# Wider records for the routing lists: rows of 64 bytes in DRAM in place of rows of 16

## The chip, the cores and the metric

The kernel runs on one core of one Trainium2 chip. The metric is the time of one execution on the device in microseconds (us). Before the change three runs took 736.26, 739.16 and 739.34 us; their median, 739.16 us, is the time before. The engines are named as in the profile: PE is TensorE, DVE is VectorE, ACT is ScalarE, POOL is GpSimd, SP is SyncE, which here only issues transfers. SPq, ACTq and POOLq are the instruction queues of those engines where they issue transfers.

## The reference

The inputs are q, k, v (4 batches, 8 heads, 576 positions, 64 wide) and the weights of two feed-forward layers. Three stages follow one another, all in float32:

```python
# 1 attention: heads 0-3 see the last 32 positions, heads 4-7 every fourth of the last 128
scores = np.where(mask, q @ k.T / 8, -1e9);  attn = softmax(scores);  x = attn @ v      # x: 2304 tokens x 512
# 2 experts: each token goes to the one expert of 8 with the largest logit
e_idx = argmax(x @ w_gate);  gate = softmax(x @ w_gate)[e_idx];  eom = sigmoid(x @ w_output_gate)
out[mask_e] = gate * eom[:, e] * (relu(x[mask_e] @ w1[e]) @ w2[e])                       # 512 -> 1024 -> 512
# 3 dense layer
h = relu(out @ w_in);  result = (h * h) @ w_out                                          # 512 -> 2048 -> 512
```

The experts run on gathered tokens: the kernel must know for every expert which tokens are its own, and with what factor.

## The kernel before, in words

**The attention stage** (function `attention`) walks over 18 tiles of 128 tokens. A loop runs over the first 15 tiles (L649), the last three are written out by hand behind it (L699 to L764). Each step of the loop loads later tiles of q, k and v on SP's queue (`load_q`, `load_k`, `load_v`), multiplies q with k (`qk`, L433), subtracts the row maximum on POOL (L454), takes the exponential on ACT (`ex`, L459), transposes (`tr`, L466), multiplies with v (`pv`, L482), normalizes on DVE (L492 to L498) and transposes the result for the gate (`xt`, L520). From step 9 on finished rows of x are stored to DRAM (`store`, L512 and L514, tensor `x_d`).

**Routing.** The tiles are taken in six groups (`GROUPS`). At the end of a group `lg` and `route1` to `route6` find each token's expert, its rank within that expert's list and its factor. `scatter` (L624) then writes one record per token into the DRAM tensor `meta_d`, which holds eight lists of MS = 2560 rows, one list per expert. A record is four 32-bit words: the token's number, the factor's bits, the token's number again, and a word not used. It is written by an indirect store on POOL's queue: a column of up to 128 tokens (one per partition) is one instruction, and the vector `di` holds for each the row of `meta_d` that it goes to. There are 20 such stores, spread over the attention stage. Their source is `idsb`, a part of the constants' tile `late_sb`, in which the token numbers lie ready and into which `route5` writes the factors (L611).

Before the first record is written, `clear` (L409) fills all of `meta_d` with zeros and, in the third word, the number OOB, so that rows that no token takes lead nowhere. It is one transfer of 320 KB on SP's queue, from a tile that POOL has filled (L642, L643), issued in the loop's step 3. The first `scatter` waits until it has landed.

**The experts stage** (function `experts`) works through nine windows, one or two per expert, in an order that is found at run time. Records are read in three places:

- `meta_load` (L153) reads a window's records into SBUF, one record per partition, and `gather` (L158) fetches the tokens' rows of x by them, with an indirect load on POOL's queue.
- `ids_out` (L855) copies a window's records from `meta_d` to the DRAM tensor `idc_d`, in the order of the experts' outputs. It is issued on ACT's queue, after the fourth of the eight `up` steps of a window (after the whole window for the first two).
- `spilled` (L1454) would read them for tokens that found no place in a window. Here it has nothing to do.

After the last window one transfer on SP's queue (L1086) reads `idc_d` into SBUF, and the 18 indirect stores of the final result (L1431) take their rows from it.

In each window `up` multiplies with w1 (12 matmuls into one of three PSUM banks `hp`, L829, then ACT and DVE take the bank out, L834 and L835) and `down` with w2 (L844, five banks `yp`). The weights come in pieces of 512 KB (`load_w`, at most three on the way, in the three `raw` buffers) and are split by ACT and DVE (`conv_w`, L143 and L144) one window ahead of their use.

**The order of the work** is written out by hand. All transfers of one issuing engine are issued in program order, and an instruction that waits holds up those behind it on its engine.

Of the kernel before, what the change touches and what calls it, by code (L numbers as in the profile page):

```python
# [13 lines left out]
I32 = mybir.dt.int32  # L14
# [9 lines left out]
P = 128  # L24
# [7 lines left out]
NG = len(GROUPS)  # L32
# [3 lines left out]
E = 8  # L36
# [5 lines left out]

HALF = EARLY * P // E
MS = NT + 256
YC = sum(WIN) + 192
NEG = -8.0e9
OOB = 65535
# [21 lines left out]
def attention_experts_kernel(ctx: ExitStack, tc: tile.TileContext, qB, kB, vB, wE, wF, consts, late, rows, out):  # L69
    nc = tc.nc  # L70
    cpool = ctx.enter_context(tc.tile_pool(name="cpool", bufs=1))
    dpool = ctx.enter_context(tc.tile_pool(name="dpool", bufs=1, space=DRAM))
# [2 lines left out]
    stg = stg_st.enter_context(tc.tile_pool(name="stg", bufs=1, side="right"))  # L75

    x_d = dpool.tile([NT, DM], F32, name="x_d")
    meta_d = dpool.tile([E * MS, 4], I32, name="meta_d")
    yT_d = dpool.tile([DM, YC], F32, name="yT_d")
    idc_d = dpool.tile([YC, 4], I32, name="idc_d")  # L80
    g_d = [dpool.tile([FF2, TP], F32, name=f"g_d{i}") for i in range(NTP)]
# [7 lines left out]
    w8 = late_sb[:, 2 * P:2 * P + 4 * E].rearrange("p (a e) -> p a e", e=E)  # L89
    eoff = late_sb[:, 2 * P + 4 * E:2 * P + 8 * E].rearrange("p (a e) -> p a e", e=E)  # L90
    idsb = late_sb[:, 2 * P + 8 * E:].bitcast(I32).rearrange("p (g b c) -> p g b c", b=4, c=4)
    cum = cpool.tile([P, NG + 1, E], BF16, name="cum")
    idc = cpool.tile([P, NT // P, 4], I32, name="idc")
    rowc = cpool.tile([1, 4 * E + E * E + NSPILL], F32, name="rowc")
# [8 lines left out]
    mt = cpool.tile([P, E + 1, 3, 4], I32, name="mt")  # L103
# [5 lines left out]
    def raw_tile():  # L109
        return stg.tile([P, 1024], F32, tag="raw", name="raw", bufs=3)  # L110
# [16 lines left out]
    reg = {}  # L127
# [25 lines left out]
    def meta_load(w, engine=None, n="p"):  # L153
        r, s0, _ = WD[w]
        k = len(tiles(w))
        (engine or nc.gpsimd).dma_start(out=mt[:, w, 0:k], in_=meta_d[ds(reg[n, r] * MS + s0, P * k), :].rearrange("(i p) c -> p i c", p=P))

    def gather(w):  # L158
        known = (NB if w else EARLY) * P
# [166 lines left out]
    def attention():  # L326
# [77 lines left out]
            nc.sync.dma_start(out=late_sb, in_=late)  # L404
            nc.sync.dma_start(out=rowc, in_=rows)

        z = raw_tile().bitcast(I32)[:, 0:MS * E * 4 // P].rearrange("p (n c) -> p n c", c=4)

        def clear():  # L409
            nc.sync.dma_start(out=meta_d.rearrange("(p n) c -> p n c", p=P), in_=z)  # L410

        sm_t, p_t, pt_t, o_t, x_t, xT_t, lg_t = {}, {}, {}, {}, {}, {}, {}

# [179 lines left out]
        def route5(g):  # L593

            ls, e, oh = rt[g]
            rk = rk_t.pop(g)
            n, c = rows_of(g), COLS[g]
            m = idsb[:, g, 0:c]
            v = nc.vector
            zp, z, ez, se, dn = t3(g, "zp"), t2(g, "z"), t2(g, "ez"), t2(g, "se"), t2(g, "dn")  # L600
            r1, s2, di = t3(g, "r1"), t2(g, "s2"), wk.tile([P, 4], I32, tag="di", name="di", bufs=4)[:, 0:c]
            v.tensor_tensor(out=zp[n], in0=oh[n], in1=ls[n, :, E:2 * E], op=ALU.mult)
            v.reduce_sum(out=se[n], in_=e[n], axis=AX.X)
            v.reduce_sum(out=z[n], in_=zp[n], axis=AX.X)
            nc.scalar.activation(out=ez[n], in_=z[n], func=ACTF.Exp, scale=-1.0)
            v.tensor_tensor(out=r1[n], in0=rk[n, 0:c], in1=eoff[n, 0:c], op=ALU.add)
            v.tensor_scalar(out=se[n], in0=se[n], scalar1=1e-9, scalar2=None, op0=ALU.add)
            v.tensor_tensor(out=r1[n], in0=r1[n], in1=oh[n], op=ALU.mult)
            v.scalar_tensor_tensor(out=dn[n], in0=ez[n], scalar=1.0, in1=se[n], op0=ALU.add, op1=ALU.mult)
            v.reduce_sum(out=s2[n], in_=r1[n], axis=AX.X)  # L610
            v.reciprocal(out=m[n, :, 1:2].bitcast(F32), in_=dn[n].unsqueeze(2))  # L611
            v.tensor_copy(di[n], s2[n])
            rt[g] = di, m, oh
# [26 lines left out]
            clear_v(j, 1, nc.gpsimd)  # L640
        nc.gpsimd.memset(cum, 0.0)
        nc.gpsimd.memset(z, 0)  # L642
        nc.gpsimd.memset(z[:, :, 2:3], OOB)  # L643
        ex(0)
        load_q(4, 2)
        load_v(2, 2)
# [2 lines left out]
        for i in range(EARLY):  # L649
            tr(i)  # L650
            ex(i + 1)
            qk(i + 2)
            t = (i + 2) % LAP
            n = i + 2 - t + LAP
            if t == 2 and n < NB:
                load_k(n, 2)
            if t == 4 and n + 2 < NB:
                wrap()
                load_k(n + 2, min(3, NB - n - 2))

            if i % 2 == 0 and i + 6 < NB:
                load_q(i + 6, 2)
            if i == 0:
                load_consts()
            if i == 3:
                clear()
            if i == 3:
                nc.vector.tensor_copy(tri, tri32)
                nc.vector.tensor_copy(cs[:, 0, :], io8)
            for a, g in ((2, ends.get(i - 2)), (4, ends.get(i - 3))):  # L670
                if g is not None and g < NG - 3:
                    scatter(g, range(a - 2, min(a, COLS[g])))
            if i > 0:
                xt(i - 1)
            g = ends.get(i - 1)
            if g is not None:
                route4(g)
            pv(i)
            if i == 0:
                for j in range(4, VR):  # L680
                    clear_v(j, 0, nc.vector)
                    clear_v(j, 1, nc.gpsimd)
                load_v(4, 2)
            if i % 2 == 1 and i + VR - 1 < NB:
                load_v(i + VR - 1, 2)
            for a in STORES.get(i, ()):
                store(a, 2)
            if i in ends:
                lg(ends[i])
                route1(ends[i])  # L690
                route2(ends[i])
                route3(ends[i])
            if g is not None:
                route5(g)
                route6(g)
                if g == NG - 3:
                    scatter(g)

        i, g = EARLY, NG - 2  # L699
# [54 lines left out]
        for t in tiles(0):  # L754
            scale(0, t)
            j, n = t
# [4 lines left out]
        n = WD[0][2]  # L761
# [4 lines left out]
    def experts():  # L766
# [88 lines left out]
        def ids_out(w):  # L855
            r, s0, n = WD[w]
            at = slice(HALF * w, HALF * w + n) if w < 2 else ds(oa[r], n)
            nc.scalar.dma_start(out=idc_d[at, :], in_=meta_d[ds(reg["a", r] * MS + s0, n), :])

# [112 lines left out]
        for w in range(NW):  # L974
            at = {i: [] for i in range(12)}
# [478 lines left out]
    def spilled():  # L1454
# [5 lines left out]
        with ExitStack() as st:  # L1460
            sp = st.enter_context(tc.tile_pool(name="sp", bufs=1))
            ps = st.enter_context(tc.tile_pool(name="sps", bufs=2, space=PSUM))
            with tc.For_i(0, total) as i:
                ev = loaded(spill[:, 0, ds(i, 1)], mybir.EngineType.SP, E - 1, "cut to the experts")[0]
                rv = loaded(spill[:, 1, ds(i, 1)], mybir.EngineType.SP, E * MS - P, "cut to the rows")[0]
                m = sp.tile([P, 4], I32, name="m")
                nc.sync.dma_start(out=m, in_=meta_d[ds(rv, P), :])
                x = sp.tile([P, DM], F32, name="sx")
                nc.gpsimd.indirect_dma_start(
                    out=x, out_offset=None, in_=x_d,  # L1470
# [5 lines left out]
                p = ps.tile([P, 4, P], F32, tag="a", name="sa")  # L1476
# [10 lines left out]
                for c in range(4):  # L1487
                    w = load_w(c).rearrange("p (k f) -> p k f", k=4)
                    for f in range(2):
                        p = ps.tile([P, P], F32, tag="a", name="sa")  # L1490
# [4 lines left out]
                for c in range(4):  # L1495
                    w = load_w(4 + c).rearrange("p (k d) -> p k d", k=8)
                    p = ps.tile([P, P], F32, tag="a", name="sa")
# [4 lines left out]
                for f in range(16):  # L1502
                    w = []
# [6 lines left out]
                    p = ps.tile([P, P], F32, tag="a", name="sa")  # L1510
                    for k in range(4):
                        nc.tensor.matmul(out=p, lhsT=wi[:, k, :], rhs=y[:, k, :], start=(k == 0), stop=(k == 3))
                    r = sp.tile([P, P], F32, tag="r", name="sr", bufs=2)
# [102 lines left out]
```

## Time and profile before

| | |
|---|---|
| median of 3 runs | 739.16 us |
| the profiled execution | 733.13 us, of which the span is 731.5 us |
| PE busy | 696.5 us (95%) |
| DVE, ACT, POOL busy | 488.0 (67%), 327.6 (45%), 116.5 us (16%) |
| transfers | 136.90 MB, 187 GB/s on average |

The profile is one execution, taken by the hardware profiler. The time outside the span is 1.6 us. The granted clock is that of TensorE, 1.00 being the upper of its two levels (2.4 GHz) and 0.50 the lower (1.2 GHz). The attention stage lasts to about 110 us of the span, the experts stage to about 350 us, the dense layer to the end. A row of the timeline view gives the start, the duration, the engine, the line, the operation, and in brackets for how long the engine had been idle before it and which work ended that wait; "issue" means that the engine waited for nothing that the profile shows.

### The profile page before, as it was taken

The page shows a single profiled execution, that of the slowest core. Times are in us where ns is not written, and L with a number is a line of the kernel's source. Part 1 is how long each engine was busy: PE and PEld are TensorE (multiplying, and loading weights), DVE is VectorE, ACT ScalarE, POOL GpSimd, SP SyncE. Part 2 cuts the span into 40 slices and gives each one's busy share as a digit, 9 for nine tenths or more (in the row PEclk, how much of TensorE's full clock was granted, in tenths as well). Part 3 has the DMA queues.
Part 4 walks back from the last instruction along what each step waited for, and adds up shares of the span by engine and source line. Part 5 has one row for each costly group of instructions (what it writes and reads, how often), then busy time and mean ns, then how long its engine had stood idle before and what let it go on. Part 6 is the DMA issues. An engine that isn't in the chain of part 4 may idle for free. (4 is left out here: it accounts for less than half of the span.)

```text
span 731.5 us, 13885 instructions
## 1 busy us (share of the span) xinstructions
PE 696.5 (95%) x5227; PEld 633.6 (87%) x5227; DVE 488.0 (67%) x898; ACT 327.6 (45%) x601; POOL 116.5 (16%) x122
## 2 busy tenths in 40 slices
PE   7978759999999999999999999999999999999995
PEld 4766529999999999999999999999988888888884
DVE  7867636677566476677986877777888854445441
ACT  2544415454455555666655555465444422222120
POOL 6354434320110101006200000000000030003003
PEclk9999869999999999999999999999999999999998
DMA  8988475673756668673537645557655443235302
GB/s 286 394 231 248 140 225 167 205 253 133 229 188 204 207 179 261 212 238 95 201 129 252 202 172 201 176 201 241 222 194 193 137 155 127 87 112 169 108 23 90
DMA packets 62307, 136.90 MB, mean 187 GB/s; under 512 B 10361, under 2 KB 37242, under 8 KB 61210
## 3 DMA queue, kind: packets, MB, share of 16 engines
q1 hardware_dynamic: 52586, 120.09, 51.1%
q0 software_dynamic: 4176, 10.57, 4.2%
q10 hardware_dynamic: 5472, 5.29, 2.1%
q8 instruction: 43, 0.70, 0.4%
q14 instruction: 30, 0.25, 0.1%
HBM read 102.00 MB, written 33.96 MB: 186 GB/s over the span
## 5 line engine op out<-in xcount | busy, mean ns | idle before, releaser
L1386 DVE TENSOR_TENSOR slot_d<-gq,slot_d 128x768 fp32r<-128x768 f32 x48 | 45.9, 957 | 63.4 <-ACT slot_d L1384 63.4
L1384 ACT CAST slot_d<-gq 128x768 fp32r<-128x768 f32 x48 | 40.0, 836 | 97.5 <-PE op L1422 90.0
L1431 POOL DMA_INDIRECT out<-os,idc x18 | 19.8, 1100 | 353.2 <-DVE os L1430 348.9
L162 POOL DMA_INDIRECT xg<-x_d,mt x23 | 25.6, 1115 | 140.6 <-PE xp L186 95.1
L834 ACT ACTIVATE hh<-hp 128x240 fp32r<-128x240 f32 (+6 forms) x72 | 29.2, 407 | 40.6 <-PE hp L822 40.0
L1377 DVE SCALAR_TENSOR_TENSOR gq<-gq 128x768 f32<-128x768 f32 x48 | 45.6, 951 | 1.0 <-DMA gq<-g_d 1.0
L144 DVE TENSOR_TENSOR slot_d<-raw,slot_d 128x1024 fp32r<-128x1024 f32 x24 | 29.3, 1226 | 19.6 <-ACT slot_d L143 19.6
L1423 PE MATMUL op<-slot_a,slot_d 128*128 128x512 f32 x108 | 42.0, 389 | 0.0
L1422 PE MATMUL op<-slot_b,slot_d 128*128 128x512 f32 x108 | 42.0, 389 | 0.0
L1423 PE MATMUL op<-slot_b,slot_d 128*128 128x512 f32 x108 | 42.0, 389 | 0.0
L1422 PE MATMUL op<-slot_a,slot_d 128*128 128x512 f32 x108 | 42.0, 389 | 0.0
L1421 PE MATMUL op<-slot_b,slot_d 128*128 128x512 f32 x108 | 42.0, 389 | 0.0
L1421 PE MATMUL op<-slot_a,slot_d 128*128 128x512 f32 x108 | 42.0, 389 | 0.0
L835 DVE SCALAR_TENSOR_TENSOR hl<-hp,hh 128x240 fp32r<-128x240 f32 (+6 forms) x72 | 31.3, 444 | 12.9 <-ACT hh L834 12.8
L849 ACT COPY ys<-yp 128x240 f32<-128x240 f32 (+6 forms) x36 | 14.2, 396 | 46.3 <-PE yp L822 43.3
L144 DVE TENSOR_TENSOR slot_b<-raw,slot_b 128x1024 fp32r<-128x1024 f32 x20 | 24.3, 1222 | 12.5 <-ACT slot_b L143 12.5
L820 PE MATMUL yp<-hh,slot_b 128*128 128x240 f32 (+3 forms) x112 | 31.9, 285 | 0.0
L821 PE MATMUL yp<-hl,slot_b 128*128 128x240 f32 (+3 forms) x112 | 31.7, 283 | 0.0
L822 PE MATMUL yp<-hh,slot_b 128*128 128x240 f32 (+3 forms) x112 | 31.6, 282 | 0.0
L144 DVE TENSOR_TENSOR slot_a<-raw,slot_a 128x1024 fp32r<-128x1024 f32 x15 | 18.3, 1223 | 18.8 <-ACT slot_a L143 18.8
L820 PE MATMUL hp<-xh,slot_d 128*128 128x384 f32 (+3 forms) x96 | 29.7, 310 | 0.0
L821 PE MATMUL hp<-xl,slot_d 128*128 128x384 f32 (+3 forms) x96 | 29.7, 309 | 0.0
(323 smaller groups left out, 2301.6 us busy)
## 6 DMA issues: line engine op xcount, KB each, us to landing
raw<-in_wE SPq DMA_DIRECT2D x63, 512.0 KB, 4.0
g_d<-cr SPq DMA_DIRECT2D x96, 192.0 KB, 2.3
gq<-g_d SPq DMA_DIRECT2D x48, 384.0 KB, 3.0
raw<-in_wF SPq DMA_DIRECT2D x32, 512.0 KB, 3.6
vb<-in_vB SPq DMA_DIRECT2D x16, 520.0 KB, 5.6
yr<-yT_d SPq DMA_DIRECT2D x16, 384.0 KB, 6.9
q<-in_qB SPq DMA_DIRECT2D x8, 512.0 KB, 7.2
x_d<-x SPq DMA_DIRECT2D x22, 128.0 KB, 6.7
```

The costliest lines, as they stand in the source:

```text
L144: nc.vector.tensor_tensor(out=lo, in0=raw, in1=hi.bitcast(F32), op=ALU.subtract)
L820: nc.tensor.matmul(out=out, lhsT=wh, rhs=mh, start=first, stop=False, skip_group_check=shared)
L821: nc.tensor.matmul(out=out, lhsT=wh, rhs=ml, start=False, stop=False, skip_group_check=shared)
L822: nc.tensor.matmul(out=out, lhsT=wl, rhs=mh, start=False, stop=last, skip_group_check=shared)
L834: nc.scalar.activation(out=h[:, :n], in_=p[:, :n], func=ACTF.Relu)
L835: nc.vector.scalar_tensor_tensor(out=l[:, :n], in0=p[:, :n], scalar=0.0, in1=h[:, :n].bitcast(F32), op0=ALU.max, op1=ALU.subtract)
L1377: nc.vector.scalar_tensor_tensor(out=x, in0=x, scalar=0.0, in1=x, op0=ALU.max, op1=ALU.mult)
L1384: nc.scalar.copy(out=h, in_=x)
L1386: return lambda: nc.vector.tensor_tensor(out=l, in0=x, in1=h.bitcast(F32), op=ALU.subtract)
L1421: nc.tensor.matmul(out=o_t[j], lhsT=h[:, a], rhs=w[:, 0], start=f == 0, stop=False)
L1422: nc.tensor.matmul(out=o_t[j], lhsT=h[:, a], rhs=w[:, 1], start=False, stop=False)
L1423: nc.tensor.matmul(out=o_t[j], lhsT=l[:, a], rhs=w[:, 0], start=False, stop=f == 15)
```

## The change

A row of `meta_d` becomes 16 words (64 bytes) in place of 4. The record's four words stand at its start, the rest is zero. So that an indirect store can write a whole row, its source becomes a new tile `idw` with 16 words per token: POOL sets it to zero, DVE copies the token numbers in from `idsb`, and `route5` writes the factors there. The tensor grows from 320 KB to 1280 KB, and `clear` with it: its source tile has the same size as before and is now read four times over. The three readers take the first four words of each row.

```diff
+MR = 16
-    meta_d = dpool.tile([E * MS, 4], I32, name="meta_d")
+    meta_d = dpool.tile([E * MS, MR], I32, name="meta_d")
+    idw = cpool.tile([P, NG, 4, MR], I32, name="idw")
@@ meta_load
-        ... in_=meta_d[ds(reg[n, r] * MS + s0, P * k), :].rearrange("(i p) c -> p i c", p=P))
+        ... in_=meta_d[ds(reg[n, r] * MS + s0, P * k), 0:4].rearrange("(i p) c -> p i c", p=P))
@@ attention
-        z = raw_tile().bitcast(I32)[:, 0:MS * E * 4 // P].rearrange("p (n c) -> p n c", c=4)
+        z = raw_tile().bitcast(I32)[:, 0:MS * E * MR // P // 4]
         def clear():
-            nc.sync.dma_start(out=meta_d.rearrange("(p n) c -> p n c", p=P), in_=z)
+            nc.sync.dma_start(
+                out=meta_d.rearrange("(p a n) c -> p a (n c)", p=P, a=4), in_=z.unsqueeze(1).to_broadcast([P, 4, MS * E * MR // P // 4])
+            )
@@ route5
-            m = idsb[:, g, 0:c]
+            m = idw[:, g, 0:c]
@@ before the loop, on POOL
         nc.gpsimd.memset(z, 0)
-        nc.gpsimd.memset(z[:, :, 2:3], OOB)
+        nc.gpsimd.memset(z.rearrange("p (n c) -> p n c", c=MR)[:, :, 2:3], OOB)
+        nc.gpsimd.memset(idw, 0)
@@ in the loop, step 3
                 nc.vector.tensor_copy(tri, tri32)
+                nc.vector.tensor_copy(idw[:, :, :, 0:4], idsb)
@@ ids_out
-            nc.scalar.dma_start(out=idc_d[at, :], in_=meta_d[ds(reg["a", r] * MS + s0, n), :])
+            nc.scalar.dma_start(out=idc_d[at, :], in_=meta_d[ds(reg["a", r] * MS + s0, n), 0:4])
@@ spilled
-                nc.sync.dma_start(out=m, in_=meta_d[ds(rv, P), :])
+                nc.sync.dma_start(out=m, in_=meta_d[ds(rv, P), 0:4])
```

No instruction changes its place. Two are added, one on POOL and one on DVE, and the shapes of three transfers change. On ACT, in the window of 328 rows, the copy of the records stood before as 16 pieces of 60 words (`hh` is what `up` leaves, `raw` and `slot_d` are weights before and after their split):

```order
L143 CAST slot_d<-raw 128x1024
L834 ACTIVATE hh<-hp 128x328 x2
L143 CAST slot_d<-raw 128x1024
L858 ISA
L858 DMA idc_d<-meta_d 16x82
L834 ACTIVATE hh<-hp 128x328 x2
L143 CAST slot_d<-raw 128x1024
```

That window's piece is 82 words long, 328 bytes; the windows of 240 rows have 60 words, 240 bytes. In the changed kernel, at the same place:

```order
L145 CAST slot_d<-raw 128x1024
L840 ACTIVATE hh<-hp 128x328 x2
L145 CAST slot_d<-raw 128x1024
L864 ISA
L864 DMA idc_d<-meta_d 328x4
L840 ACTIVATE hh<-hp 128x328 x2
L145 CAST slot_d<-raw 128x1024
```

The records no longer follow one another without gaps in `meta_d`, so the copy is one of 328 pieces of 4 words. On POOL, before the loop and in its first steps (`raw` is the clearing pattern, `sm` the scores), the changed kernel has:

```order
L645 MEMSET cum 128x56
L646 MEMSET raw 128x640
L647 MEMSET raw 128x40
L648 MEMSET idw 128x384
L458 TENSOR_TENSOR sm<-sm,mx 128x512
L377 MEMSET vb 128x1040 x2
L458 TENSOR_TENSOR sm<-sm,mx 128x512 x5
L632 DMA meta_d<-idw,di 20480x16 x2
L458 TENSOR_TENSOR sm<-sm,mx 128x512
L632 DMA meta_d<-idw,di 20480x16 x2
```

The memset of `idw` is new, the one before it writes 40 numbers per partition in place of 160, and the stores read `idw` where they read `late_sb`; their places between the subtractions of L454 (L458 after the change) are the same.

## Rows read from the trace of the kernel before

**Rows 1.** The page: the span, and PE's busy tenths in 40 slices.
```profile
span 731.5 us, 13885 instructions
PE   7978759999999999999999999999999999999995
```

**Rows 2.** Windows: stretch, its length, busy us by engine, PE clock, DMA share, GB/s.
```profile
20.00:36.00 16.00, 14.76 (x351) 11.68 (x343) 13.70 (x45) 8.45 (x22) 5.21 (x5) 1.00 1.02 398
...
42.00:44.00 2.00, 1.40 (x28) 0.84 (x23) 1.83 (x7) 0.63 (x3) 0.88 (x1) 1.00 1.40 73
44.00:46.00 2.00, 2.00 (x61) 1.77 (x55) 1.02 (x3) 1.23 (x4) 0.00 (x0) 1.00 0.69 71
46.00:48.00 2.00, 2.00 (x59) 1.53 (x48) 1.66 (x7) 0.10 (x1) 1.04 (x1) 1.00 0.77 212
...
54.00:56.00 2.00, 2.00 (x34) 1.54 (x27) 0.53 (x2) 1.09 (x2) 0.09 (x1) 0.50 0.94 62
56.00:58.00 2.00, 2.00 (x37) 1.45 (x36) 1.23 (x3) 0.65 (x2) 0.60 (x1) 0.75 0.70 204
...
74.00:76.00 2.00, 2.00 (x35) 1.67 (x28) 1.38 (x2) 1.12 (x3) 0.06 (x1) 0.52 0.65 206
76.00:78.00 2.00, 1.98 (x28) 1.29 (x20) 0.58 (x3) 0.00 (x0) 1.84 (x2) 0.63 0.59 190
```

**Rows 3.** Timeline of POOL: its wait after the memsets, and three of its rows later.
```profile
15.94 1.04 POOL L454 TENSOR_TENSOR sm<-sm,mx 128x512 f32<-128x512 f32 x1 [1.04 <-DVE mx L453]
...
36.11 1.08 POOL L628 DMA_INDIRECT meta_d<-late_sb,di  x1 [0.17 <-issue]
...
38.44 1.05 POOL L454 TENSOR_TENSOR sm<-sm,mx 128x512 f32<-128x512 f32 x1
...
51.80 1.01 POOL L628 DMA_INDIRECT meta_d<-late_sb,di  x1 [0.15 <-issue]
```

**Rows 4.** Transfers by issuing line: count, KB each, median us from issue to landing.
```profile
xg<-x_d,mt POOLq DMA_INDIRECT x23, 5.0
meta_d<-raw SPq DMA_DIRECT2D x1, 320.0 KB
meta_d<-late_sb,di POOLq DMA_INDIRECT x20, 7.6
out<-os,idc POOLq DMA_INDIRECT x18, 2.8
```

**Rows 5.** Timeline of PE, 50 to 80 us, the rows that follow a wait.
```profile
52.34 0.86 PE L482 MATMUL o<-vb,pts 128*32 128x130 f32 x19 [2.85 <-issue]
...
67.39 1.08 PE L433 MATMUL s<-kf,q 128*32 128x128 f32 x32 [0.85 <-DMA kf<-in_kB]
72.73 0.49 PE L466 MATMUL pt<-ident,pr 128*128 128x128 f32 x3 [1.94 <-issue]
78.54 1.08 PE L433 MATMUL s<-kf,q 128*32 128x128 f32 x32 [0.56 <-DMA kf<-in_kB]
```

**Rows 6.** Timeline of SP: the issue of the clearing transfer.
```profile
25.03 0.45 SPq L410 DMA_DIRECT2D meta_d<-raw  x1
```

**Rows 7.** Timelines of ACT, POOL and PE at the end of the attention stage.
```profile
98.04 1.04 ACT L143 CAST slot_a<-raw 128x1024 fp32r<-128x1024 f32 x1 [6.48 <-DMA raw<-in_wE]
...
99.05 1.05 POOL L162 DMA_INDIRECT xg<-x_d,mt  x1 [11.31 <-DMA x_d<-x]
...
101.84 0.19 PE L587 MATMUL rk<-oh,tri 128*128 128x32 bf16 x1 [6.51 <-DVE oh L578]
```

**Rows 8.** ACT's and SP's timelines late in the experts stage, and a wait of SP.
```profile
311.56 1.05 ACT L143 CAST slot_a<-raw 128x1024 fp32r<-128x1024 f32 x1 [1.18 <-DMA raw<-in_wE]
...
334.38 0.56 ACTq L858 DMA_DIRECT2D idc_d<-meta_d  x1
...
337.38 0.38 SPq L1086 DMA_DIRECT2D idc<-idc_d  x1
...
SPq L814 <- DMA yT_d<-ys: 11.9, 1, 11.9
```

More of the change, by code (lines that the diff above doesn't have):

```diff
@@ L155, in meta_load @@
         k = len(tiles(w))
-        (engine or nc.gpsimd).dma_start(out=mt[:, w, 0:k], in_=meta_d[ds(reg[n, r] * MS + s0, P * k), :].rearrange("(i p) c -> p i c", p=P))
+        (engine or nc.gpsimd).dma_start(out=mt[:, w, 0:k], in_=meta_d[ds(reg[n, r] * MS + s0, P * k), 0:4].rearrange("(i p) c -> p i c", p=P))
     def gather(w):
```

## The prediction

> **What bounds the kernel now.** I read the page first. PE's busy tenths are 9 in every slice from the seventh to the last but one; gaps stand in the first six, some 110 us [rows 1]. So the end is set by PE. In the experts and the dense layer a faster transfer can win little, while in the attention stage a wait of PE that goes shortens the whole. The changed tensor is filled there and read later: the gain, if there is one, lies in the first 110 us, and what lies behind can lose as well as win.
>
> Next I read the windows, for what the transfers reach [rows 2]. From 20 to 36 us, before the first record is stored, the 16 DMA engines are busy throughout (share 1.02) and move 398 GB/s. From 42 to 48 us the share stays between 0.69 and 1.40, but the rate falls to 73, 71 and 212 GB/s: engines that are busy and move nothing, so something holds them up. The same shows from 54 to 58 us, with 62 and 204 GB/s. Against 398 GB/s the first hole costs 6 - 2 x (73 + 71 + 212) / 398 = 4.2 us of transfer time, the second 4 - 2 x (62 + 204) / 398 = 2.7 us.
>
> POOL's timeline says what comes before each hole: indirect stores of records, four from 36.11 us on and two from 51.80 us on [rows 3]. The list of transfers compares them with other work of the same queue [rows 4]: a store of records, 128 rows of 16 bytes, lands after 7.6 us, an indirect store of the result, 128 rows of 2 KB, after 2.8 us, and an indirect load of tokens after 5.0 us. So neither the queue nor the index is slow as such; what marks the slow ones is the short row. I take it that a write of 16 bytes is only a part of what the memory writes at once, so that old content has to be read and merged, and that loads queue up behind it.
>
> Last, PE's timeline for what this costs [rows 5]. It waits 0.85 and 0.56 us for loads of k, and 2.85 and 1.94 us with no releaser in the profile ("issue"), once in the middle of a group of like matmuls. I read these two as PE's own instructions arriving late, since they come over the same DMA engines. After each the clock falls to the lower level: 0.50 and 0.75 in the four microseconds from 54 us, 0.52 and 0.63 in those from 74 us [rows 2].
>
> **The change, part by part.**
>
> *Stores of 64 bytes in place of 16.* 20 stores of up to 128 rows, at the same places. Their bytes grow fourfold to 8 KB each, which at 398 GB/s is 0.02 us and nothing. What they may win is the holes. An upper bound is all of the four waits, 2.85 + 0.85 + 1.94 + 0.56 = 6.2 us, and the lost clock, 2 x (0.50 + 0.25 + 0.48 + 0.37) = 3.2 us, together 9.4 us. The lower bound is 0; below it there is nothing, since a longer row has no more rows. The trace has no write of 64 bytes. I take the 2.85 us, which follow the first hole, with their 1.5 us of clock, less 0.4 for a remainder: 4.0; of the two waits for k (1.4) 1.0; and of the 1.94 us with their 1.7 us of clock, which lie farther from a hole, half: 1.8. Together -6.8 us, nearer to the upper end, because the holes stand so close behind the stores.
>
> *What of it reaches the end.* The gain must get through the stores of x: the first gather of tokens waits 11.31 us for one of them, and the first expert weights, which ACT awaits for 6.48 us and behind which DVE and PE stand (6.51 us), are queued behind the same stores on SP [rows 7]. These stores go through the same holes and begin earlier when the loop is earlier, so I let most pass and take off 0.6; the bounds are 0 and 6.
>
> *The clearing transfer* has 1280 KB in place of 320 [rows 4]. That is 983,040 bytes more, issued at 25.03 us [rows 6] into a stretch in which the DMA engines are full: at 398 GB/s 2.5 us more for itself and for the loads behind it. The first store of records waits for it. At present it goes off at 36.11 us with no wait for the clearing shown, and right behind it on POOL stands a subtraction that runs at 38.44 us without any wait [rows 3]; ACT's exponential, and then PE, wait for that. If clearing lands 2.5 us later, POOL can stand for as long. Bounds 0 and +2.5; I take +1.2, the middle, since no row shows how long before 36.11 us the clearing had landed.
>
> *The new tile.* The added memset of 384 numbers per partition, less 120 that another saves, lies before a wait of POOL of 1.04 us [rows 3], which covers it. The copy on DVE is one more instruction where 45 take 13.70 of 16 us, some 0.3 us each [rows 2]; its cover is the 2.3 us that DVE is idle there, and without it the cost is 0.3. Both together: 0.
>
> *The readers.* `meta_load` has as many pieces of 16 bytes as before, so 0 (bounds -0.3 and +0.3, a copy's size). `ids_out` changes: 240 to 384 records used to be 16 pieces of 240 bytes and more; now each record is its own piece of 16 bytes, written to `idc_d`. Thus the short writes do not vanish: they leave the attention stage and come back in nine transfers of the experts stage, beside weight loads. If each makes a hole like the first, reads stand still for 4.2 us nine times. The cover is large: weights are split a window ahead, and PE can go on with two of three `hp` banks while ACT waits. But late in that stage weights come just in time: ACT waits 1.18 us for one at 311.56 us [rows 8]. Bounds: 0, and 9 x 1.5 = 13.5 us (of each hole a good third comes through). I take +0.6, half of that one wait. The last `ids_out` holds up only SP's load of `idc`, and behind that SP waits 11.9 us for outputs of the experts anyway [rows 8].
>
> **Sum**: -6.8 + 0.6 + 1.2 + 0.6 = -4.4 us. Of the profiled execution, 731.5 us of span and 1.6 around it, 733.1, that leaves 728.7 us. The median of the runs, 739.16 us, is 6 us above that execution; the same step from it gives 734.8 us.
>
> **The rivals.**
>
> *The length of the row is not what counts.* It may be the number of rows, or 64 bytes may still be a part of what is written at once. For it: the trace has no row between 16 bytes and a few hundred. Against it: the last `ids_out` of before, in pieces of 240 bytes, is issued at 334.38 us, and the load that needs it goes off at 337.38 us, 3.0 us later [rows 8], against 7.6 for the stores of records. Then the gain is 0 and the costs stay: 1.2 + 0.6 = +1.8, 741.0 us. The Trainium skill has a rule for this side: "DMA: Bandwidth & Descriptors", section "Specifications", puts the least transfer for full rate at 512 bytes, and says that below it the engine reads, modifies and writes. By that rule 64 bytes would be no better than 16. The 3.0 us for pieces of 240 bytes speak against it in part; no run here shows 64.
>
> *The short writes only move, and cost more where they go* (the slower side). In the experts stage nine `ids_out` hold up the weights, ACT stands at `conv_w` with the exits of `hp` behind it, and PE runs out of banks. For it: the 1.18 us, and that every hole stands where loads are under way. Against it: the lead of a whole window. At 1.5 us each, 13.5 in all, the sum is -6.8 + 0.6 + 1.2 + 13.5 = +8.5, 747.7 us. It decides from 0.56 us per transfer (5.0 / 9), where the gain is used up.
>
> *The holes go, but the end of the attention stage stays*, because the stores of x set it: x is stored from the loop's step 9 on, and both its landing and the weights behind it are late at the end [rows 7]. Then some 1 us is left of the gain: -1.0 + 1.2 + 0.6 = +0.8, 740.0 us.
>
> **How the numbers follow.** Forecast 0.56, at 734.8, with 730 to 738 as its own range; rows that don't count by length 0.15; the moved writes 0.17; the stores of x 0.12. About 0.5%, 3.7 us, is what a measurement of this kernel can tell from no change: faster means under 735.5, slower over 742.9. Of the forecast 0.40 lies under 735.5 and 0.16 within; of the unchanged end 0.03 and 0.09; of the first rival 0.09 is within and 0.06 slower (with the clearing at its full 2.5); of the moved writes 0.02 within and 0.15 slower. That makes 0.43, 0.36 and 0.21. The range goes from 729, where most of the 9.4 us come through, to 745, which takes in the first rival whole and the moved writes up to 1.2 us each.
>
> **What would show it.** Right: no window between 40 and 60 us with a share over 0.6 and under 100 GB/s; record stores that land in under 5 us; no wait of PE over 1 us and no clock under 0.9 between 50 and 80 us; the first weights split before 95 us in place of 98.04. The clearing shows in POOL's wait before its first store. The moved writes would show in windows of low rate behind each `ids_out`, and in more and longer waits of ACT for `raw`. The forecast is wrong if the holes between 42 and 58 us stay with the longer rows, or if PE is no longer busy throughout between 130 and 340 us.

## The result and the profile after

The changed kernel takes 731.04 us (median of four runs, 729.07 to 732.81), the kernel before 739.25 us in the same comparison (four runs, 736.26 to 741.53). The ratio is 0.9894, with a 95% interval of 0.9851 to 0.9937: 8.2 us less, where the forecast was 4.4 less and 734.8. A second comparison with more runs gave 0.9905 (0.9875 to 0.9935), about 7 us. The profiled executions stand 3.85 us apart (733.13 and 729.28 us).

The first thing to look at is the rate of the transfers. Windows of the changed kernel, with the columns of [rows 2]:

```profile
42.00:44.00 2.00, 1.68 (x40) 1.13 (x33) 0.86 (x3) 0.00 (x0) 1.05 (x1) 1.00 0.88 269
44.00:46.00 2.00, 2.00 (x52) 1.68 (x54) 1.83 (x8) 1.10 (x3) 0.00 (x0) 1.00 0.99 359
46.00:48.00 2.00, 2.00 (x56) 1.63 (x52) 1.78 (x5) 0.71 (x3) 0.99 (x1) 1.00 0.89 318
...
50.00:52.00 2.00, 1.89 (x49) 1.28 (x40) 1.75 (x5) 0.84 (x2) 1.04 (x1) 1.00 0.40 107
...
54.00:56.00 2.00, 1.65 (x35) 0.95 (x32) 0.89 (x3) 0.85 (x2) 1.83 (x3) 1.00 0.69 209
56.00:58.00 2.00, 1.68 (x44) 1.54 (x45) 1.46 (x3) 0.95 (x3) 1.66 (x2) 1.00 1.05 352
...
78.00:80.00 2.00, 0.00 (x0) 0.00 (x0) 0.00 (x0) 0.01 (x1) 0.76 (x1) 0.83 0.59 190
80.00:82.00 2.00, 1.58 (x46) 1.54 (x50) 1.11 (x3) 1.22 (x3) 0.00 (x0) 0.50 0.31 100
...
90.00:92.00 2.00, 2.00 (x31) 1.52 (x24) 0.48 (x3) 0.00 (x0) 0.00 (x0) 0.50 1.02 281
```

Where before there were 73, 71 and 212 GB/s from 42 to 48 us, there are 269, 359 and 318, and from 54 to 58 us 209 and 352 in place of 62 and 204 [rows 2]. The lowest rate that is left, 107 GB/s, stands at a share of 0.40: there the DMA engines have little to do; they are not held up. The clock is 1.00 where it was 0.50 and 0.75. The three last rows show something new: PE does nothing for two microseconds, and then the clock is 0.50, up to 92 us.

PE's timeline of the changed kernel says the same from its side. The wait of 2.85 us at 52.34 us [rows 5] has no counterpart; of the wait at `tr` 1.07 us are left; and one of 4.77 us has come:

```profile
67.86 0.49 PE L470 MATMUL pt<-ident,pr 128*128 128x128 f32 x3 [1.07 <-issue]
73.74 1.08 PE L437 MATMUL s<-kf,q 128*32 128x128 f32 x32 [1.18 <-DMA kf<-in_kB]
80.42 0.96 PE L539 MATMUL lg<-xT,late_sb 128*32 128x64 f32 x26 [4.77 <-ACT xT L526]
```

The end of the attention stage in the changed kernel, from the timelines of SP, POOL, ACT and PE, answers to [rows 7]. SP issues the first weights, the first gather goes off, ACT splits the weights, PE counts ranks and then begins with the experts:

```profile
88.50 0.39 SPq L138 DMA_DIRECT2D raw<-in_wE  x1
93.17 1.05 POOL L164 DMA_INDIRECT xg<-x_d,mt  x1 [4.96 <-DVE x L502]
94.40 1.06 ACT L145 CAST slot_a<-raw 128x1024 fp32r<-128x1024 f32 x1
98.21 0.18 PE L591 MATMUL rk<-oh,tri 128*128 128x32 bf16 x1 [1.45 <-DVE oh L582]
105.16 0.38 PE L826 MATMUL hp<-xh,slot_a 128*128 128x240 f32 x1 [1.53 <-DVE xl L180]
```

Two rows of the kernel before that [rows 7] did not have, the same issue on SP and the same first matmul:

```profile
90.41 1.10 SPq L136 DMA_DIRECT2D raw<-in_wE  x1
110.27 0.38 PE L820 MATMUL hp<-xh,slot_a 128*128 128x240 f32 x1 [1.53 <-DVE xl L178]
```

In this trace the wait of 6.48 us for the first weights is gone, the gather's wait no longer ends with a store of x (in `mr8` and `mr32` below it still does, after 6.51 and 5.28 us), and the experts begin 5.1 us earlier. At the end of the span 3.9 us of it are left. Behind the attention stage PE stays busy throughout, as before; from the page:

```profile
PE   7998669999999999999999999999999999999995
```

### The profile page after: what moved, and what is told of

Same layout as the page of the kernel before. It is cut to its first block, busy times and chain, and to the rows that moved or that the text cites. A ratio compares the mean times of both kernels' runs of the same rounds, so it can differ in the third digit from the quotient of the medians.

```text
span 727.6 us, 13885 instructions
## 1 busy us (share of the span) xinstructions
PE 694.8 (95%) x5227; PEld 633.3 (87%) x5227; DVE 487.7 (67%) x899; ACT 326.5 (45%) x601; POOL 116.2 (16%) x123
## 2 busy tenths in 40 slices
DMA packets 65096, 137.99 MB, mean 190 GB/s; under 512 B 12574, under 2 KB 39647, under 8 KB 63999
## 5 line engine op out<-in xcount | busy, mean ns | idle before, releaser
L1114 ACT COPY kept<-bank_b 128x384 f32<-128x384 f32 x50 | 23.2, 486 | 14.5 <-PE bank_b L828 11.1
```

## The experiments

All ratios are to runs of the kernel before on the same chip, whose medians were 737.8, 737.7, 736.3 and 738.6 us in the four sessions. A record is 16 bytes of content everywhere.

| kernel | written per record | distance | median us | ratio, 95% interval |
|---|---|---|---|---|
| again | 64 B | 64 B | 730.86 | 0.9905, 0.9875 to 0.9935 |
| mr4 | 16 B | 16 B | 737.52 | 1.000, 0.9978 to 1.0022 |
| mr8 | 32 B | 32 B | 731.88 | 0.9917, 0.9893 to 0.9942 |
| mr32 | 128 B | 128 B | 730.98 | 0.9911, 0.9881 to 0.9942 |
| pitch64_w16 | 16 B | 64 B | 732.41 | 0.9930, 0.9901 to 0.9959 |
| pitch32_w16 | 16 B | 32 B | 733.67 | 0.9950, 0.9923 to 0.9977 |
| pitch32_again | 16 B | 32 B | 732.38 | 0.9924, 0.9892 to 0.9957 |
| no_stores | none in the loop | 64 B | 727.66 | 0.9892, 0.9835 to 0.9950 |
| clear_twice | 64 B | 64 B | 733.80 | 0.9960, 0.9937 to 0.9982 |
| idc_rows_whole | 64 B | 64 B | 732.23 | 0.9925, 0.9893 to 0.9957 |
| pe_shift | 64 B | 64 B | 729.30 | 0.9906, 0.9870 to 0.9942 |

### Is it the length of the row? (again, mr4, mr8, mr32)

`again` is the changed kernel itself. The others differ from it in one number; `mr32` also repeats its clearing tile eight times in place of four, since the tile has a fixed size.

```diff
-MR = 16
+MR = 4        # mr4;  8 in mr8;  32 in mr32
```

> The changed kernel once more, for a second trace of it. Two questions. Is the gain of 8.2 us in the medians there again (ratio .985 to .994)? And is the pause of 75 to 80 us, in which PE waits 4.77 us at 80.42 for the transposed x and the clock falls to .50 until 92, a part of the kernel or a chance of one execution? If it belongs to the kernel: the same wait of over 4 us between 74 and 82 us, span 727 to 728. If it is chance: no PE wait over 2 us between 40 and 90 us, clock 1.00 to 90, the first matmul of the experts 3 to 6 us earlier than at 105.16, and a span of 722 to 725.

> Rows of 16 bytes again, with all the rest of the change kept (separate tile of records, its memset and copy, the clear by four repeats, the column slices). Theory (short rows stall the loads): the holes are back, three windows of 2 us between 40 and 60 us under 100 GB/s with a DMA share above .5, the time is that of before, 736 to 742. Rival (the gain comes from the side effects, as the separate tile that no longer ties the records to the late constants, or from a shift in time): 729 to 733 and no holes.

> Rows of 32 bytes, written whole. Theory A (a write that is shorter than 64 bytes is a partial one, and only its number counts): the holes stay as with 16 bytes, 736 to 741. Theory B (what counts is how many records share a stretch of memory, or a cost in proportion to the missing length): the holes shrink to half, one or two windows under 100 GB/s, 733 to 736. Rival (any widening does it): no holes, 729 to 733.

> Rows of 128 bytes, written whole; the clear grows from 1280 to 2560 KB. Theory A (64 bytes are enough): no further gain in the stores, and the larger clear costs nothing up to 2 us: 730 to 734. Rival (a store of 64 bytes is still a partial one, and the remaining low windows, .40 of DMA share at 107 GB/s from 50 to 52 us, come from that): 724 to 728, and fewer PE waits between 40 and 80 us than the .3 to 1.2 us that the changed kernel shows.

`again` has the gain a second time. On the pause neither of the two answers came true: no wait of PE is over 2 us between 40 and 90 us (the longest are 1.64 us at 70.33 and 1.01 us at 80.23), and yet the clock is 0.54 and 0.50 from 82 to 88 us, the experts begin at 105.39 us, and the span is 729.4 us.

`mr4` has the new tile, its memset and copy, and the time of before: ratio 1.000. So these side effects of the change are worth nothing either way (within 0.22%, 1.6 us), and the row length is worth 737.52 - 730.86 = 6.7 us in one session. With rows of 16 bytes the clear is 320 KB again and `ids_out` moves whole pieces again (10361 packets under 512 bytes, as before the change), so the 6.7 us already have in them what these two cost; both are tried by themselves below. The windows of `mr4` show the holes again, and, behind a wait of PE of 3.95 us, the fallen clock, over six microseconds:

```profile
42.00:44.00 2.00, 1.65 (x49) 1.18 (x41) 0.74 (x4) 0.12 (x1) 1.29 (x2) 1.00 1.37 77
44.00:46.00 2.00, 2.00 (x40) 1.64 (x40) 1.83 (x8) 0.79 (x3) 0.00 (x0) 1.00 0.50 85
...
54.00:56.00 2.00, 1.69 (x20) 1.20 (x21) 0.14 (x1) 0.00 (x0) 0.96 (x1) 0.50 0.15 33
56.00:58.00 2.00, 2.00 (x28) 1.59 (x31) 0.92 (x3) 1.04 (x2) 0.00 (x0) 0.50 0.86 58
58.00:60.00 2.00, 2.00 (x33) 1.34 (x29) 1.09 (x2) 0.36 (x2) 0.00 (x0) 0.62 0.64 75
```
```profile
54.31 1.51 PE L486 MATMUL o<-vb,pts 128*32 128x130 f32 x19 [3.95 <-issue]
```

The second trace of the kernel before, `before_again`, has the same: 61 and 55 GB/s from 42 to 46 us at shares of 0.70 and 0.63, and a wait of 3.66 us at 52.54 us. In the traces with wider or more widely spaced rows no wait of PE between 45 and 60 us is longer than 0.8 us.

Rows of 32 bytes were the surprise: I had theory A at 736 to 741 and theory B at 733 to 736, and they give all of the gain, 731.88. Their trace has a window of 25 GB/s too, but at a share of 0.14; that is idle time and no hole, for SP, which issues the loads, issues none between 37.0 and 42.47 us there:

```profile
40.00:42.00 2.00, 1.75 (x34) 0.96 (x25) 0.34 (x1) 1.18 (x3) 1.35 (x2) 1.00 0.60 227
42.00:44.00 2.00, 1.68 (x47) 1.42 (x45) 1.45 (x3) 0.65 (x2) 0.00 (x0) 1.00 0.14 25
44.00:46.00 2.00, 2.00 (x40) 1.63 (x41) 1.80 (x7) 0.34 (x2) 1.04 (x1) 1.00 0.92 320
```

128 bytes bring no more than 64. The Trainium skill's page "DMA: Bandwidth & Descriptors", section "Specifications", by which everything under 512 bytes is read, modified and written, would have left 16, 32, 64 and 128 alike; here 16 side by side differ by 5.6 us from 32, and from there on nothing moves.

### Length or neighbours? (pitch64_w16, pitch32_w16, pitch32_again)

The rows stay 64 (or 32) bytes apart, and the store writes only the first 16: the tensor is seen as rows of 16 bytes, with indices four times (twice) as large.

```diff
-            v.tensor_copy(di[n], s2[n])
+            v.tensor_scalar(out=di[n], in0=s2[n], scalar1=float(MR // 4), scalar2=None, op0=ALU.mult)
...
-                    out=meta_d, out_offset=...,
-                    in_=m[n, b, :], in_offset=None, bounds_check=E * MS - 1, ...
+                    out=meta_d.rearrange("n (a c) -> (n a) c", c=4), out_offset=...,
+                    in_=m[n, b, 0:4], in_offset=None, bounds_check=E * MS * MR // 4 - 1, ...
```

> Records 64 bytes apart as in the changed kernel, but each store writes only the first 16 of them (indices four times as large into a view of rows of 16 bytes). Theory A, the length of a single write counts (16 bytes are slow wherever they go, 32 and more are not): holes as before, at least two windows of 2 us under 100 GB/s with a DMA share over .5 between 40 and 60 us, 736 to 741. Theory B, neighbours in one stretch of 32 bytes count (two records of a list lie in the same stretch and collide): no holes, 729 to 733.

> The same with records 32 bytes apart, of which 16 are written. Theory A (length of the write): holes, 736 to 741. Theory B (two records in one stretch of 32 bytes): no holes, 729 to 733. A stretch of 64 bytes that counts would show here alone: holes in this one and none with 64 bytes between the records; the rows of 32 bytes written whole speak against it.

> Records 32 bytes apart, of which 16 are written, a second time and with more runs. The first trace had one stretch of low rate (77 GB/s at a share of .90 from 42 to 44 us), and its ratio to before, .995, lay between that of whole rows of 32 bytes (.992) and of 16 bytes side by side (1.000). If two short writes into one stretch of 64 bytes still hurt: the hole again in 40 to 48 us, ratio .993 to .997. If that hole was chance: no window under 100 GB/s with a share over .6 between 40 and 60 us, ratio .990 to .993.

With 64 bytes between them, writes of 16 bytes do no harm that the trace shows: 732.41 us, and no window between 40 and 60 us under 149 GB/s. Theory A, that the length of a single write decides, has fallen. With 32 bytes between them the first hole is plain in the first trace (77 GB/s at a share of 0.90). In the second it is at the edge of what I had written down, a share over 0.6 under 100 GB/s: 0.59 at 54, then 0.67 at 111. The second hole (54 to 58 us) is in neither. A row of the first trace, then three of the second:

```profile
42.00:44.00 2.00, 1.68 (x55) 1.38 (x51) 0.81 (x3) 0.59 (x2) 1.70 (x2) 1.00 0.90 77
```
```profile
42.00:44.00 2.00, 1.73 (x47) 1.11 (x39) 1.65 (x4) 0.65 (x2) 0.39 (x2) 1.00 0.59 54
44.00:46.00 2.00, 2.00 (x50) 1.44 (x39) 1.79 (x8) 0.57 (x2) 0.89 (x1) 1.00 0.67 111
...
54.00:56.00 2.00, 1.71 (x39) 1.08 (x32) 0.30 (x1) 0.16 (x1) 1.68 (x3) 1.00 0.79 191
```

In the second trace PE loses no time by that hole: its clock stays at 1.00, and between 36 and 59 us no wait of PE is longer than 0.56. The times say less than the windows: 0.9950 and 0.9924 for the same kernel hold both answers that I had written down. The rows of 32 bytes written whole, which also lie two to 64 bytes, have no hole. So a short write alone does no harm, and neighbours alone do none; the harm is shown for 16 bytes side by side, and with 32 bytes between the records it rests on one plain trace and one at the edge. The records of one list lie side by side, and one store writes up to 128 of them. That such writes wait for one another where they share a stretch is a reading that fits; no run tries it by itself, and how long the stretch would be is left open: 32 bytes don't explain the hole of `pitch32`, and 64 explain it only if whole 32 bytes are exempt.

### Do stores of 64 bytes still cost? (no_stores)

```diff
-                if g is not None and g < NG - 3:
+                if g is not None and g < NG - 3 and a < 0:
                     scatter(g, range(a - 2, min(a, COLS[g])))
```

> The changed kernel without the 12 stores of records that the loop issues between 36 and 79 us (those of the first eleven blocks; their lists keep the cleared rows, so the experts work on row 0 in their place, in the same sizes). What do the stores of 64 bytes still cost? Theory (whole rows don't stall the loads): nothing that can be measured, 729 to 732, and the DMA windows of 40 to 60 us as in the changed kernel. Rival (they still do, in smaller holes such as .40 at 107 GB/s from 50 to 52 us): 724 to 728. For the pause of PE behind 75 us: if the stores of records or POOL's issuing of them cause it, it is gone, and the span falls by 3 to 5 us; if not, it is there, of 2 to 5 us.

The median, 727.66 us, lies in the rival's range, but the runs of the kernel before that it is compared with are quicker too (736.3 us), so the ratios decide: 0.9892 (0.9835 to 0.9950, four runs) against 0.9894 and 0.9905, and 0.9906 for `pe_shift` (below), which has all stores and is compared with the same runs. Without the 12 stores the kernel is no faster than with them, as far as this interval tells (some 4 us to either side). The window of 50 to 52 us, 107 GB/s at 0.40 in the changed kernel, is there without any store, with 66 GB/s at 0.17: the stores don't make it. A pause of PE is there (4.16 us, below); it begins at 69.7 us, before the first store that is left (71.64 us), so no store of records sets it off.

### The clear, and the copies of the lists (clear_twice, idc_rows_whole)

```diff
 # clear_twice
-            nc.sync.dma_start(out=meta_d..., in_=z...)
+            for d in (junk_d, meta_d):
+                nc.sync.dma_start(out=d..., in_=z...)
 # idc_rows_whole
-    idc_d = dpool.tile([YC, 4], I32, name="idc_d")
+    idc_d = dpool.tile([YC, MR], I32, name="idc_d")
...
-            nc.scalar.dma_start(out=idc_d[at, :], in_=meta_d[ds(reg["a", r] * MS + s0, n), 0:4])
+            nc.scalar.dma_start(out=idc_d[at, :], in_=meta_d[ds(reg["a", r] * MS + s0, n), :])
...
-        nc.sync.dma_start(out=idc, in_=idc_d[0:NT, :].rearrange("(t p) c -> p t c", p=P))
+        nc.sync.dma_start(out=idc, in_=idc_d[0:NT, 0:4].rearrange("(t p) c -> p t c", p=P))
```

> The changed kernel, with a second clear of 1280 KB into a buffer that nobody reads, issued on the same queue just ahead of the first. The prediction put the 960 KB that the change adds at +1.2 us (0 to 2.5), so 1280 KB more should cost about 1.6 us: 732.5, and POOL should wait before its first store of records at 36.3 us. If the clear lies in time that nothing waits for (rows of 32 and of 128 bytes moved 640 and 2560 KB at 731.9 and 731.0): 730 to 732, no wait of POOL.

> The changed kernel, with the lists that the experts' stage copies out kept in rows of 64 bytes too, so that those copies move whole rows and write nothing of 16 bytes; the last stage reads the first 16 bytes of each. The prediction put the copies' short writes at +0.6 us (0 to 13.5). If they cost that: 730.4 or a little less. If short writes of a plain copy stall loads as the indirect ones do: 722 to 728. If they cost nothing: 729 to 733, the same as the changed kernel.

What the clear costs is read from POOL's wait before the first store. The changed kernel and `idc_rows_whole` (1280 KB both), `mr32` (2560 KB) and `clear_twice` (two of 1280 KB), one row of POOL's timeline each:

```profile
36.27 1.08 POOL L632 DMA_INDIRECT meta_d<-idw,di  x1 [0.17 <-issue]
```
```profile
38.60 1.08 POOL L632 DMA_INDIRECT meta_d<-idw,di  x1 [0.97 <-DMA meta_d<-raw]
```
```profile
39.03 1.08 POOL L632 DMA_INDIRECT meta_d<-idw,di  x1 [3.25 <-DMA meta_d<-raw]
```
```profile
39.71 1.08 POOL L634 DMA_INDIRECT meta_d<-idw,di  x1 [3.58 <-DMA meta_d<-raw]
```

At 1280 KB POOL waits for nothing in the two traces of the changed kernel, and for 0.97 us in `idc_rows_whole`, whose clear is the same: this size is the edge. At twice as much POOL stands for 3.3 to 3.6 us. What such a wait costs in the end differs: `mr32` is at 0.9911, no slower than the changed kernel, and `clear_twice` at 0.9960, 3 to 4 us slower than `again` (by the medians and by the ratios), though only 1.6 us slower than `idc_rows_whole` on the same chip, which lies within the intervals. In `mr32` the last but one of the 18 subtractions on POOL runs at 74.55 us, between 72.73 (the changed kernel) and 74.70 (`again`): the loop had made the wait good. `clear_twice` stands at 73.61 at the same point; whether it loses anything later is not settled.

The copies with whole rows take away the writes of 16 bytes: packets under 512 bytes fall from 12574 to 10025. The time does not: 732.23 us. The short writes of `ids_out` cost nothing that can be measured (the intervals of the two ratios, 0.9925 and 0.9905, are some 2 us to either side).

### The pause behind 70 us (pe_shift, before_again)

```diff
             q = q_t.pop(i)
-            for p in range(4):
+            for p in list(range(4)) * (3 if i == 0 else 1):
```

> The changed kernel, with the first block's scores computed three times over (64 more matmuls on TensorE ahead of the loop, about 2.2 us by the 1.08 us of 32, in a stage that the loads set). They move TensorE's code by 64 matmuls and weight loads, and nothing else. If the pause behind 75 us hangs on where the code of TensorE is cut for loading, it comes at another place, or goes: another PE wait than that ahead of L539 or L486 between 74 and 83 us, or none over 1 us; without it 726 to 729, else 730 to 733. If it hangs on data or on the other engines: the same wait at the same line, 730 to 734.

> The kernel before, for a second trace of it: the profiled execution of before took 733.13 us, and the median of 25 runs of it is 737.7. If the difference is the pause behind 75 us, which all other traces show and that one does not, it is here: a wait of PE of 2 to 5 us between 76 and 88 us, the interval between the eleventh and the twelfth subtraction of L454 9 to 11 us in place of 7.5 us (75.94 to 83.45), and 736 to 739 us. If that trace was a usual one: an interval of 7 to 8 us.

The expectations count POOL's subtractions from the one at 30.82 us; their eleventh and twelfth are the last two of 18. `before_again` is the kernel before, unchanged. It took 735.12 us, and my guess about it was wrong: the interval is 7.0 us (78.44 to 85.47), as in the first trace, and the wait of 4 us is not there. But that kernel has a pause earlier, at `tr`, with the same sequel, 0.50 from 74 to 80 us. The waits of PE in `before_again`, `pe_shift` and `no_stores`, a row of each:

```profile
74.07 0.80 PE L466 MATMUL pt<-ident,pr 128*128 128x128 f32 x3 [2.77 <-issue]
```
```profile
73.71 1.41 PE L437 MATMUL s<-kf,q 128*32 128x128 f32 x32 [2.52 <-DMA kf<-in_kB]
```
```profile
73.90 1.77 PE L437 MATMUL s<-kf,q 128*32 128x128 f32 x32 [4.16 <-DMA kf<-in_kB]
```

In `pe_shift` the pause stands at `qk`, 73.71 us, where the changed kernel had it at `lg`, 80.42; the clock is 1.00 from 78 us on, and the longest later wait of PE before 92 us is 0.97 us. That the 64 matmuls move it is not shown: `no_stores`, which ran on the same chip without them, has its pause at the same `qk`, 73.90. The time, 0.9906, is that of the changed kernel, so where the pause stands is worth nothing that shows in the end. In every trace PE stands still, or nearly so, somewhere between 69 and 88 us, its longest wait there being 1.0 to 4.8 us, and 3 to 17 us of half clock follow. What makes it, the code of TensorE, the last load of k, or something behind both, is open.

## Why the prediction was right, and where it was not

**The holes go, and with them the waits that follow them.** Confirmed, by the windows and by `mr4`, which brings both back. The wait of 2.85 us and the fallen clock behind it, 4.0 of the 6.8 us, are gone whole, in every trace with wider rows.

**The two other parts of that term did not come.** The waits for k, 0.85 and 0.56 us, became one of 1.18; I had put -1.0. The wait of 1.94 us at `tr` became 1.07, but one of 4.77 us came with half clock from 80 to 92 us; I had put -1.8. "No wait of PE over 1 us and no clock under 0.9 between 50 and 80 us" is therefore not what the trace shows: 1.07 and 1.18 us, and 0.83 from 78 us on. The half that I took of this part, because it lies farther from a hole, should have been nothing: traces with holes and without have such a pause, so it belongs to this stretch of the program.

**What of it reaches the end** was the step with the wrong sign. I took 0.6 us off for the stores of x. I take the last subtraction on POOL for the end of the loop and the first matmul of the experts for the end of the stage. The first matmuls before and after are shown with the result (110.27 and 105.16 us); the subtraction before, both for `mr4`, and the subtraction after:

```profile
83.45 1.04 POOL L454 TENSOR_TENSOR sm<-sm,mx 128x512 f32<-128x512 f32 x1 [1.45 <-DVE zp L602]
```
```profile
90.52 1.04 POOL L458 TENSOR_TENSOR sm<-sm,mx 128x512 f32<-128x512 f32 x1 [4.65 <-DVE zp L606]
115.34 0.38 PE L826 MATMUL hp<-xh,slot_a 128*128 128x240 f32 x1 [1.35 <-DVE xl L180]
```
```profile
83.56 1.04 POOL L458 TENSOR_TENSOR sm<-sm,mx 128x512 f32<-128x512 f32 x1 [4.81 <-DVE zp L606]
```

From the one to the other it is 26.8 us before, 25.2 in `before_again` and 24.8 in `mr4`, but 21.6 in both traces of the changed kernel: 3 to 5 us are won behind the loop. There SP issues the stores of x and, behind them, the first weights: at 90.41 and 92.43 us before, at 95.12 in `mr4`, at 88.50 and 88.42 after; ACT splits these weights at 98.04, 98.28 and 101.08 us against 94.40 and 92.07. So the stores of x are no bound that keeps the gain: with whole rows they are through earlier, and the weights behind them too. The rival by which the end of the attention stage stays had looked at the right rows and drawn the opposite from them.

What is won within the loop differs with the trace. Against the two traces of before little is left at the last subtraction (83.56 and 83.83 us against 83.45 and 85.47): at the last but one the changed kernel leads by 3.2 and 3.7 us (72.73 and 74.70 against 75.94 and 78.44), but its pause comes only then, while theirs lies behind them. Against `mr4`, whose trace lies at its median and has the late pause too, the lead at the last subtraction is 6.7 to 7.0 us. Both executions of before that were traced took less than its median, so `mr4` is the better measure of the medians, and by it the waits in the loop count as well.

**The clearing transfer**, +1.2 us: nothing in the changed kernel, where POOL's first store waits for nothing at 36.27 us, and at most the 0.97 us of `idc_rows_whole`. The middle between 0 and 2.5 was a choice without a row; the runs put the edge at about 1280 KB.

**The copies of the lists**, +0.6 us of 0 to 13.5: nothing, by `idc_rows_whole`. As the rival had it, each of the nine copies would have made a hole. They write records side by side, 16 bytes each, and make none that shows in the time. The signs named for it don't tell the kernels apart: windows of low rate do stand behind the copies (19, 19, 54 and 84 GB/s from 2 to 4 us behind the fourth to the seventh, at shares of 0.33 to 0.57), but before has them too (32, 67, 78 and 115 at 0.28 to 0.45), and ACT's waits for `raw` between 120 and 350 us are 13.5 and 10.2 us in the two traces after, 8.3 and 10.7 before. Why a plain copy differs from an indirect store was not tried.

**The new tile**: 0, by `mr4`.

**The sum.** With the two costs of 1.2 and 0.6 at nothing, -6.2 would have been forecast from -6.8 and +0.6; 6.7 us is what the row length is worth in one session (`mr4` against `again`). That the sum fits is partly luck: the parts at the waits were too large, and the part behind the loop was missing. So it is luck, too, that the profiled execution, 729.28 us, comes so near the 728.7 of the forecast. The profiled pairs show less than the medians: 3.85 us, and 735.12 - 731.15 = 4.0 in the second pair, whose two executions are of different chips. Both executions of before, 733.13 and 735.12 us, lie in the lower part of its runs (733.15 to 741.78 in the last session), and the spans of `mr4` and `again`, 736.1 and 729.4 us, are 6.7 apart too. The trace of `mr4` has the holes and the late pause, of 4.35 us at 87.38 us; whether the longer runs of before are such ones, no trace of before shows.

**The mechanism** was right in place and wrong in part. The stores make the holes, and rows of 64 bytes end them; but that a write of 16 bytes is only a part of what the memory writes at once can't be the whole reason, since the same writes 64 bytes apart make none.

The landing of record stores in under 5 us was one of the signs, and it came true in part. The last of them is issued at 108.72 us before and at 105.10 after, and `meta_load`, which waits for it, goes off at 114.57 and 108.61 us: 5.9 and 3.5 us later. The list of transfers gives no median for the changed kernel, but it does for `pe_shift`, which has the same stores of 64 bytes; beside it `before_again`:

```profile
meta_d<-idw,di POOLq DMA_INDIRECT x20, 5.4
```
```profile
meta_d<-late_sb,di POOLq DMA_INDIRECT x20, 6.5
```

That is 5.4 us against 6.5 and 7.6 [rows 4], and still far from the 2.8 us of the result's stores: that the short row alone marks the slow stores was read too simply.

## What to carry to other kernels

Where the DMA engines are busy and the rate falls, look at which small writes were issued just before, and at whether they lie side by side. Padding the records cost no more here than a larger clear, and 32 bytes did as well as 64 or 128. Then ask which queue was late at the end of the stage: 3 to 5 us of the gain were collected there, and not at the waits within the loop. And take the traces from executions near the median: the two of before took less time than most of its runs and hid a part of the gain.

## What the runs showed of the hardware

- Indirect stores of up to 128 records of 16 bytes, side by side in DRAM, held all transfers at 73 and 77 GB/s with the DMA engines at a share of 1.40 and 1.37 (before and `mr4`, 42 to 44 us). The same writes 64 bytes apart (at least 149 GB/s between 40 and 60 us), or 32 bytes written whole (`mr8`), did not.
- Writes of 16 bytes that lie 32 bytes apart still came with a stretch of 77 GB/s at a share of 0.90 (`pitch32_w16`, 42 to 44 us), and of 54 at 0.59 and 111 at 0.67 (`pitch32_again`, 42 to 46 us); the second cost PE nothing.
- Copies from DRAM to DRAM in pieces of 16 bytes, nine of 240 to 384 pieces, cost nothing that could be measured (730.86 us with them in `again`, 732.23 with pieces of 64 bytes in `idc_rows_whole`, on two chips).
- The granted clock stayed at the lower of its two levels for 12 us (80 to 92 us of the changed kernel, 0.50) behind a pause of PE of 4.77 us, though PE was busy for 1.4 to 2.0 of every 2 us from 80 us on.
